# Dummy matmuls, wider scale matmuls and a later gate load ahead of the K projection of a DiT block

## The chip, the cores and the metric

The kernel runs on one core of one Trainium2 chip. The metric is the device time of one execution in microseconds (us). Engines are named as in the profile: PE is TensorE (matmuls; PEld its weight loads), DVE is VectorE, ACT is ScalarE, POOL is GpSimd, SP is the engine whose queue issues nearly all DMAs.

## What is computed

One diffusion transformer block on x of 2 x 256 tokens by D = 1152 columns, in bf16, with 2 heads of 576 columns and an MLP of F = 4608. A conditioning vector c (one of D columns for each of the two batches) gives six modulation vectors:

```python
mod = (silu(c) @ w_mod).reshape(B, 6, 1, D)
shift_a, scale_a, gate_a, shift_m, scale_m, gate_m = [mod[:, i] for i in range(6)]
h = layernorm(x) * (1 + scale_a) + shift_a
q, k, v = split(h @ wqkv)
a = softmax(q k^T * Dh**-0.5) v @ wo          # for each batch and head
x = x + gate_a * a
h2 = layernorm(x) * (1 + scale_m) + shift_m
return x + gate_m * (gelu(h2 @ w_fc1) @ w_fc2)
```

## The kernel before

The kernel is written by hand at the level of single instructions. A small planner (class `Sched`) records every operation with what it reads and writes. It keeps the order in which PE's and SP's operations are written down. For DVE and ACT, the first operations stand in a list written out by hand (`S.first`, L971), and the rest are put in order by the planner's own cost figures. Each instruction waits on semaphores for the operations it depends on. For PSUM (8 banks of 512 fp32 columns) dependencies are kept by whole bank, and nearly all matmuls pass through one helper (`mm`, L691), transposes through another (`tr`, L694), so that lines L692 and L695 stand for nearly all of PE's work; DMAs all have line L673.

The 512 tokens lie in four tiles of 128 (tiles 0 and 1 are batch 0, tiles 2 and 3 batch 1). D is cut into KT = 9 pieces of 128 rows for the contraction; the first KC = 5 of these pieces are treated ahead of the other four.

The work up to the K projection, in PE's order:

- seven dummy matmuls ("a", L725 to L727: identity as weights, a zeroed tile `Q4B` of 512 columns as the moving operand), then a transpose that brings c into the right layout, from which ACT and DVE make silu(c) (`ST`: 128 partitions x 18, the 9 pieces of each of 2 batches).
- five dummies ("b", L859; `warm` at L795 writes PSUM bank 2), two small matmuls (`sca_one`, L861 and L862) that write ones into the accumulators of 1 + scale_a, then the scale matmuls (`mod_kt`, L800): the contraction piece kt of the w_mod columns of scale_a times the two columns of `ST`, one matmul for each of the first five output pieces f. A matmul writes two PSUM columns, in bank 3 for f = 0 and in bank 7 for the others. The weights `WSC` come in four DMAs, of pieces 0 to 1, 2 to 4, 5 to 7, and 8.
- scale matmuls of pieces 0 and 1 (10), four dummies ("c", L865), scale matmuls of pieces 2 to 4 (15), 9 transposes of the normalised token tile 1 and 9 of tile 0 (`xn_T`, L868 and L869), the f = 0 scale matmuls of pieces 5 to 8 (4, one unit `sca_first`), and the other 16 of these pieces.
- DVE copies the first transposed piece out (`xn_T_copy`), multiplies it by its scale straight from PSUM (`hk`, L822), and copies the finished scales into `SC1A` (`sc1a`, L817). ACT copies other transposed pieces and makes the normalised tile 2 (L766), which on DVE's side needs a small operation (L764) that stands behind the copies of the scale.
- then the K projection of batch 0 (L883 on): for each of the first five pieces kt, 8 matmuls of 256 columns (`k_pair`), with transposes of tile 2 after piece 1 and those of tile 3 in two parts behind piece 4's first pairs. Each K weight piece (`WK`, 288 KB) is a DMA of its own. K of batch 1, the other four scale pieces, shift_a, and Q follow.

The loads queue on SP in the order in which they are written. Behind K and shift weights come the nine pieces of the Q weights `WQ`, with the first third of the gate_a weights (`ga_load(0)`, 864 KB) behind the second Q piece (L919 and L920); the other two thirds follow behind the Q pieces. The gate weights are read by DVE alone (`attn_gate`, L1056: 18 multiply-add passes of 1152 columns).

Of the kernel before, what the change touches and what calls it, by code (L numbers as in the profile page):

```python
# [497 lines left out]
P = 128  # L498
NTOK = 512
D = 1152  # L500
KT = 9
# [8 lines left out]
KC = 5  # L510
# [5 lines left out]
def c_mm(n):  # L516
    return max(n / 2.4 + 2.5, 27.0)
# [26 lines left out]
def build_kernel(nc, x, c, wqkv, wo, w_mod, w_fc1, w_fc2, out):  # L544
# [5 lines left out]
    with (  # L550
# [4 lines left out]
        def sb(off, nbytes, dt=BF16):  # L555
            assert off % 4 == 0 and off + nbytes <= ARENA_BYTES, (off, nbytes)
            v = arena[:, off // 2:(off + nbytes) // 2]
            if dt == F32:
                v = v.bitcast(F32)
            return v  # L560

        def ps32(bank, c0=0, n=512):
            return psum[:, bank * 512 + c0: bank * 512 + c0 + n]

        def ps16(bank, c0=0, n=1024):
            v = psum[:, bank * 512: (bank + 1) * 512].bitcast(BF16)
            return v[:, c0:c0 + n]
# [15 lines left out]
        def misc(nbytes):  # L583
            o = mo[0]
            mo[0] += (nbytes + 3) // 4 * 4
            assert mo[0] <= ARENA_BYTES
            return o
# [22 lines left out]
        Q4B = sb(O_Q4B, 1024)  # L610
# [21 lines left out]
        IDENT = sb(misc(256), 256)  # L632
        ONES = sb(misc(256), 256)
# [3 lines left out]
        ST = sb(misc(36), 36)  # L637
# [5 lines left out]
        SC1A = sb(misc(72), 72, F32)  # L643
# [27 lines left out]
        def dma(dst, src, nbytes, name, is_out=False, eng="sp", run=4096):  # L671
            eff = 1.0 if run >= 4096 else (1.08 if run >= 2304 else (1.15 if run >= 1536 else (1.3 if run >= 1024 else 1.42)))
            return S.op(eng, 500.0 if eng == "sp" else 150.0, lambda e: e.dma_start(dst, src), reads=[src], writes=[dst],  # L673
                        name=name, dma_bytes=nbytes * eff, is_out=is_out)

        def dve(cost, fn, reads, writes, name):
            return S.op("dve", cost, fn, reads=reads, writes=writes, name=name)
# [7 lines left out]
        def copy_on(eng, dst, src, n, psum16, name):  # L685
            if eng == "act":
                act(c_act(n), lambda e: e.activation(out=dst, in_=src, func=ACTF.Copy), [src], [dst], name)  # L687
            else:
                return dve(c_dve_psum16(n) if psum16 else c_dve_psum32(n), lambda e: e.tensor_copy(dst, src), [src], [dst], name)  # L689

        def mm(o, l, r, st, sp, **kw):  # L691
            S.instr(lambda e: e.matmul(o, lhsT=l, rhs=r, start=st, stop=sp, **kw), reads=[l, r], writes=[o])  # L692

        def tr(o, i_, idn):  # L694
            S.instr(lambda e: e.transpose(o, i_, idn), reads=[i_, idn], writes=[o])  # L695
# [59 lines left out]
        for t in range(4):  # L755
# [5 lines left out]
            m = MV[:, t, 0:1]  # L761
# [14 lines left out]
        def xt_ps(b, kt, n=1):  # L776
            if b == 0:
                return (4, 5, 6)[kt // 4], (kt % 4) * 256
            return (7, (kt - KC) * 256) if kt >= KC else ((6, 4)[kt % 2], kt // 2 * 256)

        def xn_T(t, part="", kts=range(KT)):
            b = t // 2
            S.unit("pe", len(kts) * c_mm(128), "xnT_%d%s" % (t, part))
            for kt in kts:
                bank, c0 = xt_ps(b, kt)
                tr(ps16(bank, c0 + (t % 2) * 128, 128), XN[:, t, kt * 128:(kt + 1) * 128], IDENT)

        def xn_T_copy(b, kts, eng):
            bank, c0 = xt_ps(b, kts[0])
            n = len(kts)  # L790
            src = ps16(bank, c0, n * 256).rearrange("p (k t) -> p k t", k=n)
            st = kts[1] - kts[0] if n > 1 else 1
            copy_on(eng, HX[:, kts[0]:kts[-1] + 1:st, b * 256:(b + 1) * 256], src, n * 256, True, "xnT_cp%d_%d" % (b, kts[0]))

        def warm(n, tag):  # L795
            for i in range(n):
                S.unit("pe", 215.0, "warm_%s_%d" % (tag, i))
                mm(ps32(2), IDENT, Q4B, True, True)

        def mod_kt(W, kt, col0, name, fs=(0, 9)):  # L800
            if name:
                S.unit("pe", (fs[1] - fs[0]) * 27.0, name)
            for f in range(*fs):
                mm(ps32(7 if f else 3, col0 + f * 2, 2), W[:, kt, f * 128:(f + 1) * 128], ST[:, kt:18:9], False, kt == KT - 1,
                   skip_group_check=True)

        def quads(w, g0, g1, q):
# [7 lines left out]
                   skip_group_check=not fresh)  # L815

        def sc1a(ka, kb):  # L817
            m, o = ps32(7 if ka else 3, 2 * ka, 2 * (kb - ka)), SC1A[:, 2 * ka:2 * kb]
            dve(170, lambda e: e.tensor_copy(o, m), [m], [o], "sc1a_%d" % ka)


        def hk(kt, b, eng="dve"):  # L822
            dst, s1 = HK[:, kt, b * 256:(b + 1) * 256], SC1A[:, kt * 2 + b:kt * 2 + b + 1]
            if kt + b == 0:
                s1 = ps32(3, 0, 1)
            bank, c0 = xt_ps(b, kt)
            src = ps16(bank, c0, 256) if kt < KC and kt + b > 0 else HX[:, kt, b * 256:(b + 1) * 256]
            if eng == "act":
                act(c_act(256, 1), lambda e: e.activation(out=dst, in_=src, func=ACTF.Copy, scale=s1), [src, s1], [dst], "hk_%d_%d" % (kt, b))
                return  # L830
            dve(256 if kt < KC else 200, lambda e: e.tensor_scalar(out=dst, in0=src, scalar1=s1, scalar2=None, op0=ALU.mult),
                [src, s1], [dst], "hk_%d_%d" % (kt, b))
# [10 lines left out]
        def k_pair(kts, i, b, bank=None):  # L843
            S.unit("pe", 2 * len(kts) * c_mm(256), "k%d_%d_%d" % (b, i, kts[0]))
            bank = KB[b][i] if bank is None else bank
            if kts[0] == 0:
                for kt in kts:
                    for half in range(2):
                        k_mm((kt,), 2 * i + half, b, bank, half)
            else:  # L850
                for half in range(2):
                    k_mm(kts, 2 * i + half, b, bank, half)
            if kts[-1] == KT - 1:
                eng = "act" if ev_rr[0] % 2 == 0 else "dve"
                ev_rr[0] += 1
                copy_on(eng, QK[:, 9 + 2 * i:11 + 2 * i, b * 256:(b + 1) * 256], ps32(bank).rearrange("p (j t) -> p j t", j=2), 512, False,
                        "k_ev%d_%d" % (b, i))

        warm(5, "b")  # L859
        S.unit("pe", 27.0, "sca_one")  # L860
        mm(ps32(7, 0, 2 * KC), ONES[0:1, :], ONES[0:1, 0:2 * KC], True, False, skip_group_check=True)  # L861
        mm(ps32(3, 0, 2), ONES[0:1, :], ONES[0:1, 0:2], True, False, skip_group_check=True)  # L862
        for kt in range(0, 2):
            mod_kt(WSC, kt, 0, "sca_%d" % kt, (0, KC))
        warm(4, "c")  # L865
        for kt in range(2, 5):
            mod_kt(WSC, kt, 0, "sca_%d" % kt, (0, KC))
        xn_T(1)  # L868
        xn_T(0)  # L869
        S.unit("pe", 4 * 27.0, "sca_first")  # L870
        for kt in range(5, 9):
            mod_kt(WSC, kt, 0, "", (0, 1))
        xn_T_copy(0, (0,), "dve")
        hk(0, 0)
        sc1a(0, 1)
        for kt in range(5, 9):
            mod_kt(WSC, kt, 0, "sca_%d" % kt, (1, KC))
        sc1a(1, KC)
        for kt in range(1, KC):
            hk(kt, 0, "act" if kt == 4 else "dve")  # L880
        xn_T_copy(0, (8,), "act")
        xn_T_copy(0, (5, 6, 7), "act")
        for kt in range(KC):  # L883
            for i in range(2 if kt == KC - 1 else 4):
                k_pair((kt,), i, 0)
            if kt == 1:
                xn_T(2)
# [15 lines left out]
        for c0, c1 in ((0, 32), (32, 32 * (KT - KC))):  # L903
            ka, kb = KC + c0 // 32, KC + c1 // 32
# [9 lines left out]
        def ga_load(k0):  # L914
            dma(WMODR[:, k0:k0 + 3, 0:FG], wmod_v[:, k0:k0 + 3, 2 * D:2 * D + FG], 3 * P * FG * 2, "ld_ga%d" % k0, run=FG * 2)

        for kt in range(KT):
            dma(WQ[:, kt, :], wqkv_v[:, kt, 0:D], P * D * 2, "ld_wq%d" % kt, run=2304)
            if kt == 1:  # L919
                ga_load(0)  # L920
        for kt in range(KC, KT - 2):
            for b in range(2):
# [225 lines left out]
        def acc_bank():  # L1148
            b = acc[acc_rr[0] % len(acc)]
            acc_rr[0] += 1  # L1150
            return b
# [125 lines left out]
        for t in range(4):  # L1277
# [4 lines left out]
            for (c0, c1) in pieces:  # L1282
                w = c1 - c0
                S.unit("pe", JT * c_mm(w), "fc2_%d_%d" % (t, c0))
                o = ps32(acc_bank(), 0, w)
# [22 lines left out]
def bass_standalone__dit_block__diffusion_kernel(  # L1308
    nc: bass.Bass,
    x: bass.AP,  # L1310
    c: bass.AP,
    wqkv: bass.AP,
    wo: bass.AP,
    w_mod: bass.AP,
    w_fc1: bass.AP,
    w_fc2: bass.AP,
    out: bass.AP,
):
    build_kernel(nc, x, c, wqkv, wo, w_mod, w_fc1, w_fc2, out)
# [28 lines left out]
```

## Time and profile before

| what | value |
|---|---|
| time, median of 3 runs | 242.92 us (242.85 to 243.38) |
| the profiled execution's span, first to last instruction | 242.5 us |
| the runs' median over that span | 0.4 us |
| mean granted PE clock | 0.993 of full speed |
| PE busy | 237.3 us, 98% of the span |
| DVE, ACT, POOL busy | 121.5, 67.8, 19.9 us |
| DMA, mean over the span | 213 GB/s; 370 to 413 GB/s in the first ten slices after the first |

How to read it: the profile is of one execution, whose own time is not listed beside its span; the medians of runs stand 0.4 us over the span. All times inside the execution count from the span's start. A matmul's listed length contains its passage through the array, so back-to-back matmuls overlap in the list, and their pitch (start to start) is what one of them costs in a row of others. PEclk is the granted share of PE's full clock.

### The profile page before, as it was taken

Reading aid. Unit: us, or ns where it says so; the run is one execution under the profiler, and the core shown is the slowest. Engines: PE = TensorE matmul, PEld = TensorE weight load, DVE = VectorE, ACT = ScalarE, POOL = GpSimd, SP = SyncE. Lnnn points to the kernel's source line nnn. Section 1 sums busy time; section 2 is a strip of 40 time slices with the busy share of each in tenths; the row PEclk is TensorE's granted clock in tenths of the full one; section 3 lists DMA queues with packets and bytes.
Section 4 is the critical chain, followed back from the end, with each engine's and each line's share of the span. In section 5 each row is a group of like instructions: output and inputs, shape, how many; then the busy total and the mean of one; then the engine's idle time right before and its main releaser. Section 6 shows DMA issues by size and latency. Waiting matters only on the chain.

```text
span 242.5 us, 3957 instructions
## 1 busy us (share of the span) xinstructions
PE 237.3 (98%) x1699; PEld 145.4 (60%) x1699; DVE 121.5 (50%) x229; ACT 67.8 (28%) x136; POOL 19.9 (8%) x36
## 2 busy tenths in 40 slices
PE   6899999999999999999999999999999999999995
PEld 2688844466666666898544444444666566566564
DVE  2654379988996689669999700000022222111112
ACT  4921440435524206973233322222000000000000
POOL 1300000000002276400000110000000000000000
PEclk9979999999999999999999999999999999999999
DMA  6999999999992999999963499100000000000000
GB/s 221 378 370 392 389 392 390 398 413 402 391 352 79 312 374 391 391 348 398 352 198 83 157 313 374 43 0 3 0 16 19 16 16 16 19 16 16 21 27 20
DMA packets 30363, 51.58 MB, mean 213 GB/s; under 512 B 1547, under 2 KB 15755, under 8 KB 30347
## 3 DMA queue, kind: packets, MB, share of 16 engines
q1 hardware_dynamic: 29888, 50.73, 58.9%
q0 software_dynamic: 288, 0.60, 0.8%
q8 instruction: 13, 0.21, 0.4%
q10 hardware_dynamic: 171, 0.01, 0.0%
q14 instruction: 3, 0.02, 0.0%
HBM read 50.15 MB, written 1.19 MB: 212 GB/s over the span
## 4 chain that ended last, share of the span: by engine, by line
PE 95%; DMA 3%; SPq 1%; DVE 0%; issue 0%
PE psum L692 93%; DMA arena<-in_wqkv_dram 3%; PE psum L695 2%; SPq L673 1%; DVE arena L1290 0%; DVE arena L1291 0%
## 5 line engine op out<-in xcount | busy, mean ns | idle before, releaser
L692 PE MATMUL psum<-arena 128*128 128x384 bf16 (+8 forms) x1610 | 234.0, 314 | 2.4 <-POOL arena L718 1.5
L692 PEld LDWEIGHTS psum<-arena 128*128 128x128 bf16 (+2 forms) x1610 | 139.7, 97 | 92.4 <-issue 3.8
L1290 DVE TENSOR_TENSOR arena<-psum,arena 128x384 f32<-128x384 f32 (+2 forms) x13 | 6.8, 526 | 88.6 <-PE psum L692 88.6
L1200 ACT ACTIVATE arena<-psum 128x512 bf16<-128x512 f32 (+1 forms) x45 | 22.8, 512 | 42.1 <-PE psum L692 42.1
L687 ACT ACTIVATE arena<-psum 128x512 bf16<-128x512 f32 (+6 forms) x34 | 18.2, 560 | 37.9 <-PE psum L692 37.9
L1064 DVE SCALAR_TENSOR_TENSOR arena<-arena 128x1152 f32<-128x1152 bf16 x16 | 21.9, 1408 | 0.0
L1095 DVE SCALAR_TENSOR_TENSOR arena<-arena 128x1152 f32<-128x1152 bf16 x16 | 21.4, 1414 | 0.0
L1166 POOL TENSOR_TENSOR arena<-arena 128x384 f32<-128x384 f32 x12 | 10.9, 912 | 11.7 <-DVE arena L1165 9.5
L740 DVE BATCH_NORM_STATS2 arena<-arena 128x6 f32<-128x384 f32 (+1 forms) x18 | 9.5, 549 | 3.8 <-DMA arena<-in_x_dram 3.8
L673 POOL DMA_DIRECT2D dit_scratch<-arena x4 | 2.4, 609 | 96.6 <-DVE arena L1082 60.3
L689 DVE CAST arena<-psum 128x512 bf16<-128x512 f32 x11 | 7.2, 687 | 5.3 <-PE psum L692 5.3
L1165 DVE TENSOR_TENSOR arena<-psum,arena 128x384 f32<-128x384 f32 x12 | 6.7, 556 | 3.7 <-PE psum L692 3.7
L1171 ACT ACTIVATE arena<-arena 128x1152 bf16<-128x1152 f32 x4 | 5.4, 1344 | 9.8 <-DVE arena L1170 9.8
L695 PE MATMUL psum<-arena 128*128 128x128 bf16 (+1 forms) x89 | 7.4, 225 | 0.4 <-DMA arena<-in_c_dram 0.4
L695 PEld LDWEIGHTS psum<-arena 128*128 128x128 bf16 (+1 forms) x89 | 6.3, 102 | 2.2 <-DMA arena<-in_c_dram 1.1
L1291 DVE TENSOR_TENSOR arena<-arena 128x384 bf16<-128x384 f32 (+2 forms) x13 | 6.9, 527 | 0.5
L1190 ACT ACTIVATE arena<-psum,arena 128x128 bf16<-128x128 bf16 x16 | 6.1, 455 | 3.0 <-PE psum L695 2.2
L1187 DVE TENSOR_SCALAR arena<-psum,arena 128x128 bf16<-128x128 bf16 x20 | 5.5, 336 | 2.9 <-PE psum L695 2.9
L1009 ACT ACTIVATE arena<-psum,arena 128x256 bf16<-128x256 f32 x8 | 3.7, 471 | 0.2 <-DVE arena L1006 0.2
L744 POOL TENSOR_TENSOR arena<-arena 128x1 f32<-128x1 f32 x6 | 3.3, 555 | 4.7 <-DVE arena L743 4.5
L1005 DVE TENSOR_REDUCE arena<-psum 128x2 f32<-128x512 f32 x4 | 2.8, 688 | 0.9 <-PE psum L692 0.7
L962 ACT ACTIVATE arena<-arena 128x256 bf16<-128x256 bf16 x6 | 2.5, 495 | 1.5 <-DVE arena L956 1.5
(60 smaller groups left out, 53.9 us busy)
## 6 DMA issues: line engine op xcount, KB each, us to landing
arena<-in_w_fc_dram SPq DMA_DIRECT2D x9, 1152.0 KB, 8.0
arena<-in_w_fc_dram SPq DMA_DIRECT2D x4, 2592.0 KB, 17.6
arena<-in_wqkv_dram SPq DMA_DIRECT2D x18, 288.0 KB, 9.3
arena<-in_w_mod_dram SPq DMA_DIRECT2D x6, 864.0 KB, 12.3
arena<-in_w_mod_dram SPq DMA_DIRECT2D x3, 1728.0 KB, 20.5
arena<-in_wqkv_dram SPq DMA_DIRECT2D x1, 2592.0 KB, 17.6
arena<-in_wo_dram SPq DMA_DIRECT2D x1, 2592.0 KB, 24.9
arena<-in_w_mod_dram SPq DMA_DIRECT2D x1, 2592.0 KB, 18.5
```

Source lines behind the costliest of these rows:

```text
L687: act(c_act(n), lambda e: e.activation(out=dst, in_=src, func=ACTF.Copy), [src], [dst], name)
L689: return dve(c_dve_psum16(n) if psum16 else c_dve_psum32(n), lambda e: e.tensor_copy(dst, src), [src], [dst], name)
L692: S.instr(lambda e: e.matmul(o, lhsT=l, rhs=r, start=st, stop=sp, **kw), reads=[l, r], writes=[o])
L695: S.instr(lambda e: e.transpose(o, i_, idn), reads=[i_, idn], writes=[o])
L740: dve(550, lambda e, s=s, o=o: e.bn_stats(out=o, in_=s), [s], [o], "bn_%s_%d" % (tag, ci))
L1064: ga_units[(b, kt)] = dve(150 + FG * 1.1, lambda e, o=o, w=w, s1=s1: e.scalar_tensor_tensor(out=o, in0=w, scalar=s1, in1=o, op0=ALU.mult, ...
L1095: u = dve(1300, lambda e, o=o, w=w, s1=s1: e.scalar_tensor_tensor(out=o, in0=w, scalar=s1, in1=o, op0=ALU.mult, op1=ALU.add), [w, s1, o], ...
L1165: dve(550, lambda e, o=o, ga=ga, x1c=x1c: e.tensor_tensor(out=x1c, in0=o, in1=ga, op=ALU.mult), [o, ga], [x1c], "wo_t1_%d_%d" % (t, ci))
L1166: S.op("pool", 930, lambda e, xs=xs, x1c=x1c: e.tensor_tensor(out=x1c, in0=x1c, in1=xs, op=ALU.add), reads=[x1c, xs], writes=[x1c], name=" ...
L1200: act(c_act(ntok), lambda e: e.activation(out=dst, in_=o, func=ACTF.Gelu_apprx_tanh), [o], [dst], "gelu_%d_%d" % (f, tok0))
L1290: dve(c_dve_psum32(w), lambda e, o=o, gm=gm, t1=t1: e.tensor_tensor(out=t1, in0=o, in1=gm, op=ALU.mult), [o, gm], [t1], "fc2_t1_%d_%d" % ( ...
L1291: dve(c_dve_32(w), lambda e, t1=t1, x1c=x1c, ost=ost: e.tensor_tensor(out=ost, in0=t1, in1=x1c, op=ALU.add), [t1, x1c], [ost], "fc2_out_%d ...
```

## The change

The change has four parts.

- Each scale matmul of the first five output pieces takes its two moving columns 32 times over, 64 columns in all, and writes 64 PSUM columns for each f instead of 2; the two matmuls that write the ones become 320 and 64 columns wide. The copies of the finished scales pick the first two columns of each group of 64.
- Nine more dummy matmuls of 512 columns: three more in "c", two behind the transposes of tile 1 ("e"), two behind those of tile 0 ("f"), one inside `sca_first` before its last scale matmul, and one directly ahead of K ("d").
- The first third of the gate_a weights is loaded behind the fifth Q piece instead of the second.
- Nothing else: the hand-written order of DVE and ACT is the same list.

```diff
             for f in range(*fs):
-                mm(ps32(7 if f else 3, col0 + f * 2, 2), W[:, kt, f * 128:(f + 1) * 128], ST[:, kt:18:9], False, kt == KT - 1,
+                mm(ps32(7 if f else 3, f * 64, 64), W[:, kt, f * 128:(f + 1) * 128], ST[:, kt:18:9].unsqueeze(1).broadcast_to([P, 32, 2]), False, kt == KT - 1,
                    skip_group_check=True)
...
         def sc1a(ka, kb):
-            m, o = ps32(7 if ka else 3, 2 * ka, 2 * (kb - ka)), SC1A[:, 2 * ka:2 * kb]
+            m = ps32(7 if ka else 3, 64 * ka, 64 * (kb - ka)).rearrange("p (f c) -> p f c", c=64)[:, :, 0:2]
+            o = SC1A[:, 2 * ka:2 * kb].rearrange("p (f c) -> p f c", c=2)
             dve(170, lambda e: e.tensor_copy(o, m), [m], [o], "sc1a_%d" % ka)
...
-        mm(ps32(7, 0, 2 * KC), ONES[0:1, :], ONES[0:1, 0:2 * KC], True, False, skip_group_check=True)
-        mm(ps32(3, 0, 2), ONES[0:1, :], ONES[0:1, 0:2], True, False, skip_group_check=True)
+        ones64 = ONES[0:1, 0:64].unsqueeze(1)
+        mm(ps32(7, 0, 64 * KC), ONES[0:1, :], ones64.broadcast_to([1, KC, 64]), True, False, skip_group_check=True)
+        mm(ps32(3, 0, 64), ONES[0:1, :], ONES[0:1, 0:64], True, False, skip_group_check=True)
         for kt in range(0, 2):
             mod_kt(WSC, kt, 0, "sca_%d" % kt, (0, KC))
-        warm(4, "c")
+        warm(7, "c")
         for kt in range(2, 5):
             mod_kt(WSC, kt, 0, "sca_%d" % kt, (0, KC))
         xn_T(1)
+        warm(2, "e")
         xn_T(0)
+        warm(2, "f")
         S.unit("pe", 4 * 27.0, "sca_first")
         for kt in range(5, 9):
             mod_kt(WSC, kt, 0, "", (0, 1))
+            if kt == 7:
+                mm(ps32(2), IDENT, Q4B, True, True)
...
         xn_T_copy(0, (5, 6, 7), "act")
+        warm(1, "d")
         for kt in range(KC):
...
             dma(WQ[:, kt, :], wqkv_v[:, kt, 0:D], P * D * 2, "ld_wq%d" % kt, run=2304)
-            if kt == 1:
+            if kt == 4:
                 ga_load(0)
```

## The prediction

> **What bounds the kernel now.** I read the page first, then the table of stretches, the list of events in order of time, and the chain of waits.
>
> ```profile
> PE 237.3 (98%) x1699; PEld 145.4 (60%) x1699; DVE 121.5 (50%) x229; ACT 67.8 (28%) x136; POOL 19.9 (8%) x36
> PEclk9979999999999999999999999999999999999999
> PE 95%; DMA 3%; SPq 1%; DVE 0%; issue 0%
> 3.77 6.99 DMA arena<-in_wqkv_dram
> 10.81 3.31 PE psum L692 x16
> ```
>
> TensorE (PE) is busy for 98% of the span. The third slice (12 to 18 us) has a clock of 0.7 where the others have 0.9 or more. The chain of waits runs over the landing of the first K weight tile (issued at 3.77, 6.99 us later landed, so 10.76) and then over PE alone to the end: from 10.81 on nothing but PE sets the end. A microsecond won or lost ahead of that point, or in the K stage, is therefore worth a microsecond at the end as long as nothing else becomes late.
>
> The table of stretches (start:end, length, then busy time of each engine, then PEclk, DMA share, GB/s) shows the third slice more closely:
>
> ```profile
> 4.32:7.73 3.41, 2.96 (x23) 1.18 (x22) 2.68 (x10) 3.19 (x6) 0.99 (x3) 1.00 0.99 339
> 7.73:11.15 3.42, 2.67 (x58) 2.37 (x58) 2.12 (x10) 2.91 (x7) 0.87 (x2) 1.00 1.04 389
> 11.15:14.56 3.41, 3.41 (x22) 2.60 (x20) 2.60 (x8) 1.64 (x2) 0.25 (x1) 0.50 1.06 388
> 14.56:17.97 3.41, 3.41 (x40) 3.08 (x38) 1.35 (x5) 0.58 (x2) 0.30 (x1) 1.00 1.09 363
> ```
>
> For exactly one stretch of 3.41 us the granted clock is 0.50, right behind a stretch in which PE had little to do. What it did there is in the list of events (start, length, count, idle time before):
>
> ```profile
> 6.80 1.02 PE L692 MATMUL psum<-arena 128*128 128x512 bf16 x4
> 8.35 0.55 PE L692 MATMUL psum<-arena 128*128 128x2 bf16 x15 [0.53 <-DMA arena<-in_w_mod_dram]
> 8.76 1.17 PE L695 MATMUL psum<-arena 128*128 128x128 bf16 x18
> 9.76 0.88 PE L692 MATMUL psum<-arena 128*128 128x2 bf16 x20
> 11.04 3.08 PE L692 MATMUL psum<-arena 128*128 128x256 bf16 x14
> 13.90 0.98 PE L695 MATMUL psum<-arena 128*128 128x128 bf16 x9
> ```
>
> A listed length contains the tail of the last matmul, so I work with the pitch, start to start. Four dummies: (1.02 - 0.378)/3 = 0.214 us. Eighteen transposes of 128 columns: (1.17 - 0.219)/17 = 0.056. Fifteen scale matmuls of 2 columns: (0.55 - 0.165)/14 = 0.027. K matmuls of 256 columns at full clock: 0.109; in the slow stretch 0.213. So the dummies stop streaming at 7.66, then PE waits for scale weights until 8.35 (0.69 us), streams almost nothing in the 2-column matmuls, waits 0.20 us for the last scale tile (start 10.05) and 0.30 us for K (10.81).
>
> **The clock term.** The K stage's first two tiles and the transposes of token tile 2 (16 matmuls, 9 transposes) take from 10.81 to the first matmul of K tile 2 at 14.72, 3.91 us. At full clock they take 16 x 0.109 + 9 x 0.056 = 2.25 us. The slow stretch costs 1.66 us (check: 3.41/2 = 1.71).
>
> Does the change remove it? I count streamed time in each stretch. Before, 7.73:11.15 has 18 x 0.053 of transposes and 0.33 of K matmuls, 1.3 us (38%; 10% without the transposes), and the clock fell. 4.32:7.73 has about 2.1 us of dummies (61%), and it held. After the change, between 7.73 and 11.15: dummies 0.6 (rest of "c") + 0.86 ("e", "f") + 0.21, 64-column scale matmuls some 24 x 0.027 = 0.65, transposes 0.96: 3.3 us, 96%. Leaving the transposes out it is 68%, leaving out the wider scale matmuls as well 49%. The dummies stream zeros, but so did the seven at the start, after which the clock was full. So I take it that the clock holds.
>
> **The added work.** Nine dummies are 9 x 0.214 = 1.93 us. The price of a 64-column scale matmul has no row: the 2-column ones have a pitch of 0.027 and the 80-column ones of the last output piece 0.036 (33 listed from 238.83 on); I take 0.029, on the line through 128, 256 and 512 columns. Its moving operand repeats two columns 32 times, which no row shows, so the upper end is that of 128 columns, 0.056; the lower is 0.027. The wider initial matmul (320 columns, 0.13 us) falls into the wait for scale tiles 0 and 1 (they land at 6.47).
>
> Step by step: scale tiles 0 and 1 from 6.52, 10 x 0.029, then seven dummies from 6.82 to 8.32. The next weights are usable at 8.35, so the three dummies added to "c" are hidden in the old wait; they are 0.03 us from costing. 15 scale matmuls to 8.80; 9 transposes to 9.30; "e" to 9.73; 9 transposes to 10.23; "f" to 10.66; three first-column matmuls, the dummy and the fourth to 10.99 (its weights landed at 10.00); 16 remaining scale matmuls to 11.46; "d" to 11.67. K starts there, if its input is ready. That input: the last first-column matmul ends at 11.15, the DVE multiply (0.29 us, 10.36 before) then runs 11.19 to 11.48, usable by about 11.55. So K starts at 11.67 on PE's own account, **0.86 us later** than 10.81. By ends: 0.79 at 0.027; 2.0 at 0.056, where the first ten, too, push "c" 0.24 us past 8.35 (35 x 0.027 + 0.24 = 1.2 more). A gain below nothing is excluded, for each added column still streams.
>
> **What is late next.** Weights: the K tiles 1 to 4 land at 11.50, 13.02, 13.77 and 14.53 (issue plus landing time), and are now wanted at 12.5, 13.9, 14.8 and 15.7: covered by 0.9 us or more. The vector copies of the scale wait for the last scale matmul (end 11.6), so the normalisation factor of tile 2 follows at about 12.0 instead of 11.04 and ACT's 1.35 us pass over tile 2 ends at 13.3 to 13.4; its transposes are wanted at 11.67 + 1.75 = 13.42. This is the tightest edge: 0 to 0.1 us, I take 0.03. DVE's statistics of tile 3 start at 12.7 instead of 12.29, so its halves are normalised at 15.7 and 16.1, wanted at 16.1 and 16.6: covered. The strided copies of the scale read 2 and 8 elements as before (0.15 and 0.17 us): nothing.
>
> **The gate load.** All later work of PE now comes about 0.8 us earlier, and I looked for loads that were closer than that. One was: the third Q tile lands at 33.25 and would be wanted at 33.1. The move puts the three Q tiles ahead of a gate load that takes 2.25 us of the queue (30.24 to 32.49), so that tile lands at about 31.0 and the gate at 34.75. The gate's first reader is DVE, after the hx additions and one copy:
>
> ```profile
> 34.52 0.68 DVE L689 CAST arena<-psum 128x512 bf16<-128x512 f32 x1
> 35.12 1.54 DVE L1061 TENSOR_SCALAR arena<-arena 128x1152 f32<-128x1152 bf16 x2
> 36.58 8.06 DVE L1064 SCALAR_TENSOR_TENSOR arena<-arena 128x1152 f32<-128x1152 bf16 x6
> 45.14 1.29 DVE L689 CAST arena<-psum 128x512 bf16<-128x512 f32 x2 [0.51 <-PE psum L692]
> ```
>
> Those would move to 34.3; waiting until 34.8 delays them by 0.5 us against PE, and the 0.51 us that DVE sat idle ahead of 45.14 hides that. The queued copies behind them are not wanted earlier. I price the move at nothing; with that cover gone it costs up to 0.4 us on DVE, off PE's chain. The other six gate tiles and all later loads keep their place.
>
> **Sum.** -1.66 + 0.86 + 0.03 = -0.77 us, on a span of 242.5. The runs' median of 242.92 lies 0.4 us over that span, so I forecast 242.92 - 0.77 = **242.1 us** (span 241.7).
>
> **The rivals.**
> *The clock falls anyway* (slower side). If what is counted is not what I count, the stretch 11.15:14.56 stays at 0.50 and the added work alone remains: 242.92 + 0.86 = 243.8. It decides if the strict count of 49% is too little; against it stands the 96%, and that dummies alone raised the clock at the start. The Trainium skill, "TensorE: Matmul & The Clock Gate", Part 4 (PE-mode transpose), says that transposes do not count as activity the way matmuls do; by that rule the count is 68%, still over the 61% that held here, and no run here has yet shown it. Chance 0.14.
> *The repeated columns stream slowly.* At 0.056 each K starts 1.2 us later still: 243.3. Nothing in the profile shows such an operand. Chance 0.08.
> *K is fed late*: the edge at tile 2, or DVE behind it, costs 0.3 to 0.5 us: 242.5. The margins above are thin but were worked from rows. Chance 0.12.
> *The slow stretch isn't tied to the kernel.* If stretches began elsewhere in other executions, some runs before would lose nothing and take 241.3; the change would then take 242.1 still and gain nothing on average. The three times before span 0.53 us, where such runs would differ by 1.66: chance 0.05. (The same page of the Trainium skill, Part 1, calls the 3.4 us window free-running; the three times do not show it.)
> *The forecast*: 0.61, between 241.8 and 242.4.
>
> **How the numbers follow.** Two runs can be told apart from about 0.2%, 0.49 us. Faster by more: the forecast's case and a little of the third, 0.62. Within: most of late feeding, of the free stretch and of slow columns, 0.22. Slower: the falling clock and a little of slow columns, 0.16. The range leaves out the falling clock and little else, and reaches to the upper bound of the columns: 241.7 to 243.3.
>
> **What would show it.** The stretch 11.15:14.56 at clock 1.00; the first K matmul near 11.67 and tile 2's first near 13.95; 64-column scale matmuls at a pitch of 0.029; no wait between 8.35 and 11.67; the third Q tile landed near 31. A clock of 0.50 anywhere after 4.32, or K starting past 12.0, makes it wrong.

## The result

The changed kernel takes 245.08 us (median of 4 runs, 244.85 to 245.91) against 242.90 (4 runs, 242.85 to 243.38): ratio 1.0095, 95% interval 1.0078 to 1.0113. It is 2.2 us slower where 0.8 us faster was forecast. The profiled execution has a span of 244.2 us and a time of 245.91, so the time lies 1.7 us over the span.

The page of the changed kernel: PE's busy time, and the chain that ended last.

```profile
PE 239.3 (98%) x1699; PEld 146.8 (60%) x1708; DVE 121.2 (50%) x229; ACT 67.9 (28%) x136; POOL 20.2 (8%) x36
PE 97%; DMA 2%; issue 0%; DVE 0%; ACTq 0%
```

PE is still what ends last, and it is busy 2.0 us longer although the stretch at half clock is gone. This trace holds no record of the clock, so its share is printed as 1.00 throughout, and the pitches have to tell it. The table of stretches of the changed kernel (start:end, length, busy time of PE, PEld, DVE, ACT, POOL, then PEclk, DMA share, GB/s):

```profile
7.73:11.15 3.42, 3.42 (x43) 2.59 (x42) 1.19 (x4) 1.90 (x4) 1.28 (x2) 1.00 1.03 376
11.15:14.56 3.41, 3.36 (x42) 2.66 (x41) 1.08 (x6) 1.24 (x3) 0.00 (x0) 1.00 1.05 393
```

PE's events in order of time, in the changed kernel (start, length, count):

```profile
5.12 2.31 PE L692 MATMUL psum<-arena 128*128 128x512 bf16 x5
8.29 1.67 PE L692 MATMUL psum<-arena 128*128 128x512 bf16 x7
9.80 1.04 PE L692 MATMUL psum<-arena 128*128 128x64 bf16 x15
10.68 0.67 PE L695 MATMUL psum<-arena 128*128 128x128 bf16 x9
14.15 0.93 PE L692 MATMUL psum<-arena 128*128 128x256 bf16 x7
16.40 2.35 PE L692 MATMUL psum<-arena 128*128 128x256 bf16 x20
```

Three things stand there. The five dummies of the second group run at half clock: (2.31 - 0.63)/4 = 0.42 us each, where in the first profile of before they had 0.216. The fifteen 64-column scale matmuls have a pitch of (1.04 - 0.22)/14 = 0.059 us, with the clock full on either side (dummies (1.67 - 0.378)/6 = 0.215, transposes 0.056). And K starts at 14.15 instead of 10.81. From there the K stage runs at full clock: K piece 2 starts 2.25 us behind the first K matmul (16.40), as forecast.

### The profile page after: what moved, and what is told of

Its sections match the earlier page's. It is cut to its first block, busy times and chain, and to the rows that moved or that the text cites. A ratio compares the mean times of both kernels' runs of the same rounds, so it can differ in the third digit from the quotient of the medians.

```text
span 244.2 us, 3966 instructions
## 1 busy us (share of the span) xinstructions
PE 239.3 (98%) x1699; PEld 146.8 (60%) x1708; DVE 121.2 (50%) x229; ACT 67.9 (28%) x136; POOL 20.2 (8%) x36
## 4 chain that ended last, share of the span: by engine, by line
PE 97%; DMA 2%; issue 0%; DVE 0%; ACTq 0%
PE psum L692 95%; PE psum L695 2%; DMA arena<-in_c_dram 2%; ACTq L673 0%; DVE arena L1297 0%; DVE arena L1298 0%
## 5 line engine op out<-in xcount | busy, mean ns | idle before, releaser
L692 PE MATMUL psum<-arena 128*128 128x384 bf16 (+7 forms) x1610 | 236.3, 315 | 2.1 <-POOL arena L718 1.5
L692 PEld LDWEIGHTS psum<-arena 128*128 128x128 bf16 (+2 forms) x1619 | 141.4, 97 | 92.4 <-issue 4.8
```

## The experiments

Theory A, formed on the result: the half-clock stretch is not part of a usual execution of the kernel before, so there is nothing to win; the changed kernel pays the added PE time, less the waits of PE that it fills. Rival B: each execution of the kernel before pays the stretch, as its profile did, and the wide scale matmuls ate the gain. All ratios below are to the kernel before, timed alongside.

### Both kernels again

> The kernel before, run and profiled again. Theory A (the slow clock stretch of 3.41 us between 11.15 and 14.56 is not tied to the kernel; most executions do not have it): the time lies some 1.7 us over the span, as it does for the changed kernel (245.91 against 244.2), so the timed runs at 242.9 have spans near 241.2, mean clock near 1.00, and the first profile with 242.5 and 0.993 was of an execution that is not typical. Rival B (each execution pays the stretch): spans stay near 242.5 with a mean clock of 0.993, and K tile 2 starts near 14.7 again.

> The changed kernel, run and profiled again. Both theories: 2.2 us slower than before (245.1), scale matmuls of 64 columns at a pitch of 0.059 us wherever the clock is full. Theory A adds that the point at which the clock becomes full, between 6.8 and 8.3 in the first profile against 4.32 in that of before, moves from execution to execution, and with it the start of K (14.15 in the first profile, about 13.1 when the clock is full by 5). Rival B: the late clock is a property of this kernel and shows at the same place again.

Measured, before again: 243.08 us (12 runs), ratio 1.0007 (0.9995 to 1.0018). The profiled execution has a span of 241.4. Its page first:

```profile
PEclk9999999999999999999999999999999999999999
PE 94%; DMA 3%; SPq 1%; issue 0%; DVE 0%
```

Its table of stretches:

```profile
7.73:11.15 3.42, 3.06 (x60) 2.46 (x59) 2.16 (x10) 3.02 (x7) 0.94 (x2) 1.00 1.03 377
11.15:14.56 3.41, 3.15 (x33) 2.63 (x32) 2.48 (x8) 1.58 (x2) 0.00 (x0) 1.00 1.05 393
```

And PE's events, from the last scale matmuls on (idle time before, and what ended it, in brackets):

```profile
9.99 0.60 PE L692 MATMUL psum<-arena 128*128 128x2 bf16 x17 [0.20 <-DMA arena<-in_w_mod_dram]
10.76 1.05 PE L692 MATMUL psum<-arena 128*128 128x256 bf16 x8 [0.16 <-DMA arena<-in_wqkv_dram]
12.06 1.03 PE L692 MATMUL psum<-arena 128*128 128x256 bf16 x8 [0.26 <-DMA arena<-in_wqkv_dram]
13.47 2.36 PE L692 MATMUL psum<-arena 128*128 128x256 bf16 x20
```

No slice below 9, no stretch at 0.50, and K waits for its weights instead (0.26 us of shown idle time ahead of 12.06, 0.43 by the pitch). Of the 88 executions of the kernel before that were timed as the base of the runs below, up to `after_third`, 5 had a mean clock of 0.993; they took 244.2 to 244.5 us. (One of the 12 of `before_again` itself is a sixth: 244.6 us.) The others had 0.999 or 1.000, spans of about 241.2, and the median of about 242.9. The first profile of before, with 242.5 and 0.993, was thus of one of the rare executions. Rival B is out.

The changed kernel again: 245.62 (6 runs), ratio 1.0109 (1.0088 to 1.0129), pitch 0.059 again. Its clock is recorded as full from 7.05, before's from 4.32 in one profile and 6.21 in the other. In the kernel before the point moves, as Theory A had it. The changed kernel has it late in both of its profiles so far, as rival B had it for this kernel; its third one, `after_third` below, has it at 4.85, so there the point moves too.

### The two parts alone

Wide scale matmuls alone (`wide_only`: the diff of lines L804, L818 and L861) and the nine dummies alone (`dummies_only`: the `warm` lines and the one in `sca_first`).

> The kernel before with the 64-column scale matmuls alone: no added dummies, the gate load where it was. 45 scale matmuls at 0.059 instead of 0.027 are 1.44 us; the first ten (0.32) hide in the 0.69 us wait for scale weights, and some of the other 1.12 in the waits of 0.20 and 0.30 us ahead of the last scale tile and of K. Theory A: 0.6 to 0.9 us slower than before. Rival B (the clock stretch is always paid, and activity removes it): the wider matmuls raise the activity of 7.73 to 11.15 by about 1.4 us, the stretch goes, and the kernel is 0.8 to 1.0 us faster.

> The kernel before with the nine added dummies alone, scale matmuls of 2 columns. The three in the first group hide in the 0.69 us wait; the other six are 1.29 us, less the waits of 0.20 and 0.30 us that they fill. Theory A: 0.8 to 1.1 us slower than before. Rival B: the stretch at half clock goes (1.66 us) and the kernel is 0.6 to 0.9 us faster.

Measured: 243.68 us, ratio 1.0031 (1.0019 to 1.0044), and 243.70 us, ratio 1.0036 (1.0023 to 1.0049): 0.75 and 0.87 us slower by the ratios. Both lie in Theory A's ranges and on the other side from rival B's. (The medians differ by 0.67 and 0.69, the second just below its range.) Together the parts cost more (2.3 to 2.6 us) than the sum of both alone (1.6), since each alone fills the same waits.

### Three edits that were priced at nothing, and four dummies

```diff
-            if kt == 1:                 # gate_only
+            if kt == 4:
...
-        warm(4, "c")                    # c_only
+        warm(7, "c")
...
+        warm(2, "e")                    # ef_only, behind xn_T(1)
+        warm(2, "f")                    # behind xn_T(0)
```

> The kernel before with the later gate load alone. Priced at nothing: within 0.2 us of before (243.0), DVE's first gate pass starting at about 34.8 instead of 34.0. If the load order matters to Q, up to 0.2 us faster; if the gate's chain matters, up to 0.5 us slower.

> The kernel before with the three dummies added to the third group alone, those that were priced as hidden in the 0.69 us wait for scale weights. If that wait is there in most executions (the clock full at 4.3): within 0.1 us of before. If the clock becomes full only at about 6.2, as in the second profile of before, the wait is 0.06 us and the three push all that follows by 0.6 us; the waits behind them (0.34, 0.30, 0.43 us in that profile) then take it up, and the time is within 0.2 us of before all the same.

> The kernel before with the four dummies among the first transposes alone, 0.86 us of PE work. Theory A: the waits of PE behind them (0.34 + 0.30 + 0.43 us and 0.14 before the transposes of tile 3 in the second profile of before) take them up: 0 to 0.2 us slower, where the prediction's working put each of them on the chain. Rival: each dummy behind 8.35 is paid, 0.86 - 0.5 = 0.36 us or more.

Measured: `gate_only` 1.0003 (0.9985 to 1.0021), DVE's first gate pass at 34.72; `c_only` 1.0007 (0.9995 to 1.0020); `ef_only` 1.0011 (0.9999 to 1.0022). The first two cost nothing that can be measured. The third is 0.27 us by its ratio, between the two expectations: inconclusive, though clearly below the 0.86 us of PE work that it adds.

### Why a 64-column scale matmul costs 0.059 us

Five forms of the moving operand, everything else as in `wide_only` except that the copy of the finished scales picks its columns to match:

```diff
-ST[:, kt:18:9].unsqueeze(1).broadcast_to([P, 32, 2])                    # wide_only: a b a b ..., 18 bytes apart
+ONES[:, 0:64]                                                           # wide_contig: 64 in a row
+ST[:, kt:18:9].unsqueeze(2).broadcast_to([P, 2, 32])                    # wide_inner: a x 32, then b x 32
+ONES[:, 0:2].unsqueeze(1).broadcast_to([P, 32, 2])                      # pair_near: a b a b ..., 2 bytes apart
+ST[:, kt:18:9].unsqueeze(1).unsqueeze(3).broadcast_to([P, 16, 2, 2])    # pair_twice: a a b b ..., 18 bytes apart
```

> As wide_only, but the 64 moving columns are contiguous ones in place of the two silu(c) columns repeated; this leaves out the real scale_a of the first five pieces. Theory P (the layout of the operand, two columns 18 bytes apart read 32 times, sets the pitch of 0.059): the pitch falls to 0.027 to 0.031, the kernel is within 0.2 us of before. Rival Q (64 columns cost 0.059 in this place whatever they hold, for instance by the weight loads beside them): 0.059 again, 0.6 us slower.

> As wide_only, but each of the two columns is repeated 32 times in a row (the operand steps 0 bytes 31 times, then 18 bytes) instead of the pair 32 times over; the scales are computed as in the reference. Theory P1 (the jump at each column costs): pitch 0.027 to 0.031, time within 0.2 us of before. Theory P2 (any operand that is not contiguous costs): 0.059 and 0.6 us slower.

> As wide_only, the pair of columns again taken 32 times over, but the two lie side by side (two ones, 2 bytes apart) instead of 18 bytes apart; this leaves out the real scale_a of the first five pieces. If the distance between successive columns sets the pitch of 0.059: 0.030. If going back and forth does, at any distance: 0.059. The Trainium skill, SBUF (State Buffer), Door 1, has lines of 16 bytes in which successive accesses are cheap: by it 0.030.

> As wide_only, the two columns 18 bytes apart, each taken twice before the jump to the other (16 times over); the scales are computed as in the reference. If each jump of 18 bytes costs the same: half as many jumps, a pitch near 0.044. If two accesses in one place are enough to hide the jump, as the same section of the Trainium skill says of its 16-byte lines: 0.030.

PE's fifteen scale matmuls of pieces 2 to 4 in `wide_only`, then in `wide_inner`, in `wide_contig`, in `pair_near` and in `pair_twice`:

```profile
8.64 1.05 PE L692 MATMUL psum<-arena 128*128 128x64 bf16 x15
```

```profile
8.65 0.61 PE L692 MATMUL psum<-arena 128*128 128x64 bf16 x15 [0.67 <-DMA arena<-in_w_mod_dram]
```

```profile
8.72 0.61 PE L692 MATMUL psum<-arena 128*128 128x64 bf16 x15
```

```profile
8.63 0.64 PE L692 MATMUL psum<-arena 128*128 128x64 bf16 x15 [0.42 <-DMA arena<-in_w_mod_dram]
```

```profile
8.46 0.66 PE L692 MATMUL psum<-arena 128*128 128x64 bf16 x15 [0.33 <-DMA arena<-in_w_mod_dram]
```

(1.05 - 0.22)/14 = 0.059, and (0.61 - 0.19)/14 = 0.030 twice; `pair_near` has (0.64 - 0.19)/14 = 0.032 and `pair_twice` (0.66 - 0.20)/14 = 0.033. So neither the 64 columns nor the repetition costs, but each single access that jumps 18 bytes; two accesses ahead of each jump hide it. That is what the Trainium skill, "SBUF — State Buffer", Door 1, says of 16-byte lines that want at least two hits each (18 bytes apart, two columns never share one); the trace agrees (0.059 with one, 0.030 to 0.033 with two or more). `wide_inner` computes the same scales at no cost: ratio 0.9995 (0.9979 to 1.0011); `wide_contig` 1.0001 (0.9985 to 1.0017). The other two were timed once each, 243.35 and 243.21 us beside 243.45 of the kernel before.

Two of these profiles bear on the clock as well. In `wide_inner` and `pair_near` it became full at 4.17 and 4.29, next to the 4.32 of the first profile of before. Both have the 64-column matmuls but none of the nine dummies. Their next stretch of 3.41 us, at full clock, streams more than the 38% (10% without the transposes) behind which the clock fell there: in `wide_inner` 59% and 31%, an estimate from the pitches. The stretch after that, first in `wide_inner`, then in `pair_near`, is still at 1.00:

```profile
10.99:14.40 3.41, 3.33 (x43) 2.83 (x39) 2.80 (x11) 2.10 (x3) 0.00 (x0) 1.00 1.04 395
```

```profile
11.12:14.53 3.41, 3.25 (x35) 2.75 (x34) 2.66 (x9) 1.98 (x3) 0.00 (x0) 1.00 1.05 393
```

With one execution each, this suggests that the added streaming holds the clock, but does not show it.

### The changed kernel with the better layout

The `wide_inner` edit in the changed kernel.

> The changed kernel with one edit: each of the two moving columns repeated 32 times in a row, which alone brought the pitch from 0.059 to 0.030. Theory A (added PE time less the waits that it fills): 45 x 0.029 = 1.3 us less PE work than the changed kernel, all of it on the chain because the waits are filled already; 0.6 to 0.9 us slower than before where the changed kernel is 2.2 to 2.7 slower, so the layout costs twice as much here as the 0.67 us that it cost alone. Rival (costs add up one by one): 2.2 - 0.67 = 1.5 us or more slower.

Measured: 244.41 us (6 runs, 243.49 to 244.58), ratio 1.0054 (1.0041 to 1.0066), 1.3 us slower than before. The layout alone is worth some 1.0 to 1.3 us here, close to the full 45 x 0.029 = 1.3, more than the 0.75 it cost alone. But the level lies between the two expectations, above Theory A's 0.6 to 0.9. In the profile the scale weights landed late, at 7.58 (first scale matmul at 7.63), and that was paid too; whether it was so in the other five runs is not shown.

### A late start, absorbed or paid

```diff
-        warm(5, "b")
+        warm(2, "b")   # after_b2, on the changed kernel
+        warm(8, "b")   # before_b8 and after_b8
```

> The changed kernel with two dummies instead of five in the second group, ahead of the ones (the clock becomes full during or behind that group). Theory A (a late full clock is paid in full by the changed kernel, since its three to five dummies at half clock, 0.43 us each, push the first scale matmul from 6.5 to 7.5): the first scale matmul starts at 6.5 to 6.7 in each execution, the time falls by 0.5 to 1.0 us, to 1.2 to 1.8 us over before, and the spread of spans (243.1 to 245.1) narrows to some 0.6 us. Rival (spread and level come from the landing of loads): within 0.3 us of the changed kernel, spread as wide.

Measured: 244.79 us, four runs at 244.73 to 244.80 and two at 246.18 and 246.71; ratio 1.0098 (1.0073 to 1.0123). The expectation failed by the ratio, and the spread did not narrow; the four runs that lie together are at the fast end of the changed kernel's (244.80 to 246.86). The profile is of the slowest run (246.71). There the clock became full only at 10.16, so that about five of the seven "c" dummies ran at half clock instead of those in front:

```profile
8.05 2.70 PE L692 MATMUL psum<-arena 128*128 128x512 bf16 x7
```

Seven at full clock took 1.67 us in the changed kernel. Whether the missing dummies moved that point is not shown: one profile has it, and four of the six runs are too fast to have lost as much.

> The kernel before with eight dummies instead of five in the second group, so that the first scale matmul starts 0.3 to 1.2 us later than 6.5. Theory A: the waits behind it take that up, as the three profiles do in which the first scale matmul starts at 6.52, 6.96 and 7.07 and K at 10.81, 10.76 and 10.75; K near 10.8 to 11.2, 0 to 0.3 us slower than before. Rival (a late start is paid by any of these kernels): 0.5 us or more slower.

> The changed kernel with the same three dummies added in the second group. Theory A: from the first scale matmul to K it has no wait left (6.46 us in both profiles of it), so the later start is paid in full: first scale matmul at 7.4 to 8.5, K 6.46 us behind it, 0.4 to 0.9 us slower than the changed kernel of this call. Rival: within 0.3 us of it.

> The changed kernel once more, beside the two others. Both theories: 2.0 to 2.7 us slower than before; K 6.46 us behind the first scale matmul.

Measured: `before_b8` 1.0002 (0.9990 to 1.0014), `after_third` 245.73 us, 1.0100 (1.0079 to 1.0120), `after_b8` 245.90 us, 1.0114 (1.0094 to 1.0134). The kernel before absorbs the delay, as expected. The changed one lost only 0.2 us, within the rival's 0.3 and less than Theory A had it, and the two profiles say why. In `after_b8` the scale weights landed at 6.48, and the eight dummies set the first scale matmul (7.65). In `after_third`, with five, PE was ready by 6.6 but the weights landed at 7.37 (first scale matmul at 7.42). So the comparison itself started late, and the times alone don't decide between the two; the 6.46 us from there to K does, for it held in both.

The profiles taken together, starts in us:

| profile | first scale matmul | first K matmul | tile 3's transposes | span | span less tile 3 |
|---|---|---|---|---|---|
| before, first (half clock) | 6.52 | 10.81 | 16.91 | 242.5 | 225.6 |
| before_again | 6.97 | 10.76 | 15.80 | 241.4 | 225.6 |
| gate_only | 7.07 | 10.75 | 15.31 | 240.9 | 225.6 |
| before_b8 | 7.12 | 11.24 | 15.82 | 241.4 | 225.6 |
| c_only | 6.95 | 11.17 | 15.64 | 241.6 | 226.0 |
| wide_only | 7.18 | 11.71 | 16.27 | 241.9 | 225.6 |
| dummies_only | 6.73 | 11.73 | 16.21 | 241.8 | 225.6 |
| after_inner | 7.63 | 12.76 | 17.20 | 242.8 | 225.6 |
| after | 7.69 | 14.15 | 18.58 | 244.2 | 225.6 |
| after_again | 7.51 | 13.97 | 18.40 | 244.0 | 225.6 |
| after_third | 7.42 | 13.88 | 18.31 | 243.9 | 225.6 |
| after_b8 | 7.65 | 14.11 | 18.54 | 244.1 | 225.6 |
| after_b2 | 7.45 | 14.95 | 19.38 | 245.0 | 225.6 |

Whatever is done at the head, the rest takes 225.6 us in these profiles and in the five not listed. The one exception is `c_only`, where PE waits once more, for a load of w_mod weights that landed at 19.70:

```profile
19.74 1.43 PE L692 MATMUL psum<-arena 128*2 128x128 bf16 x21 [0.26 <-DMA arena<-in_w_mod_dram]
```

In the three profiles of the changed kernel and the one of `after_b8`, K starts 6.46 us behind the first scale matmul each time: there is no wait left between them, and a late start is paid in full. In those of the kernel before it is 4.29, 3.79 and 3.68 (the first two rows and `gate_only`): K starts at 10.75 to 10.81 wherever the scales began, 0.05 to 0.07 behind the landing of the first K weights (10.76, 10.71, 10.68).

With that the loss adds up, between `before_again` and `after_again`: nine dummies at 0.2155 are 1.94 us, 45 scale matmuls at 0.032 more each are 1.44; the waits that PE had between 6.97 and 15.80 were 0.06 + 0.34 + 0.30 + 0.43 + 0.03 + 0.14 = 1.30 (each the start less what the pitch lets expect); the first scale matmul is 0.54 later. 1.94 + 1.44 - 1.30 + 0.54 = 2.62, and the spans differ by 2.6. Of the 0.54, 0.13 are the wider matmuls that write the ones (0.26 us from their start to the first scale matmul instead of 0.13). The other 0.41 are the five dummies ahead of them, at half clock until 7.05 in one execution and until 6.21 in the other: that part is not the change's own.

None of these kernels beat the kernel before: `wide_inner`, `gate_only`, `c_only` and `before_b8` are level with it within their intervals, and no run pointed to a faster one.

## Why the prediction was wrong

- **What bounds the kernel** was right: PE alone from the K stage on, and a microsecond at the head is one at the end.
- **The clock term, -1.66 us, failed.** The step that failed is "The runs' median of 242.92 lies 0.4 us over that span", which set the profiled execution beside the timed ones as if it were like them. The time lies 1.7 us over the span in every run of which both are listed, so the profiled execution would have taken about 244.2 and was no sample of the median. The rival that named this got a chance of 0.05 on the ground that the three times differed by only 0.53 us; that showed them to be alike, not to be like the profile. Also the term's size: executions with the stretch take 1.5 us more (244.4 against 242.9), since at full clock K is held up by its weights, which landed at 11.93 and 13.42 in `before_again`.
- **The clock holds after the change**: none of the 16 runs of the changed kernel has a mean clock below 1.00, though a trace without a clock record gives 1.00 too; in its three profiles the pitches from the "c" dummies into the K stage are those of the full clock. With 5 in 88 before, that does not show that the added activity did it, nor which instructions count as activity: that stays open. The two profiles shown with the layouts speak for it, without showing it.
- **The pitch of the scale matmuls, 0.029, was mis-sized**: 0.059, just over the upper end of 0.056 that I had drawn from 128 columns. A line through contiguous operands says nothing about one that jumps. This is 45 x 0.030 = 1.35 us.
- **The nine dummies** were sized right (0.2155 each). **The three hidden in "c"** were not hidden in the changed kernel: "c" ran from 8.29 to about 9.80, and the weights that it should have waited for land at 8.19. The cover of 0.03 us had depended on a first scale matmul at 6.52, one execution's value; it is at 7.42 to 7.69 in the profiles of the changed kernel. The 0.13 us of the wider matmul of ones, put at nothing because they would fall into the wait for scale weights, were paid in the first two of these profiles: the weights had landed at 6.53 and 7.07, and this matmul started at 7.37 and 7.25.
- **K at 11.67** became 14.15. **The tightest edge** (tile 2's transposes) came to nothing: with K so late, they follow K directly at 15.90.
- **The gate load at nothing** was right; the third Q tile landed at 31.39 against 31.0 forecast.
- **The rivals** were priced as if one excluded the other. Slow columns (1.2 us more) and a stretch that isn't tied to the kernel both held; 242.92 + 0.86 + 1.2 = 245.0 is what came. The agreement is partly luck, as the filled waits and the late start had other sizes.

## What to carry to other kernels

Before a stall in one profile is counted as a gain, see whether that execution is like the timed ones: compare its time, or its span plus what lies around the span in other runs, with the median. Work put into idle time of an engine is free only until the waits are filled, and each part of a change fills the same waits; from then on every late load and late clock in front of it is paid in full. Price an operand by its access pattern, not only by its number of columns, and let rivals hold together.

## What the runs showed of the hardware

- A moving operand whose successive columns jump 18 bytes streams 64 columns at a pitch of 0.059 us; with two accesses ahead of each jump, or columns 2 bytes apart, 0.032 to 0.033; contiguous or repeated in a row, 0.030. At half clock (the first ten of `after_b2`, from 7.45 to 8.00, between dummies at half clock) the jumping form has 0.060, hardly more than at full clock.
- The moment at which the clock becomes full moves between executions: 4.17 to 7.05 us in the ten profiles that record it and have the same first twelve dummies, 10.16 in the one with three fewer. The Trainium skill, "TensorE: Matmul & The Clock Gate", Part 1, calls the 3.4 us window by which the clock is set free-running, and the traces agree. A stretch of 3.41 us at half clock follows in one profile of the kernel before, and by the mean clock in 5 of 88 of its executions.
- Loads move too: the first scale weights landed at 6.27 to 7.58 us over these profiles.
